# A product's sign, swap and add on GpSimd, handed out one piece per unit

## The chip, the cores and the metric

The kernel runs on one core of one Trainium2 chip. The metric is the device time of one execution in microseconds (us), the median of several runs. Before the change it was 2526.43 us in three runs (2524.81, 2526.43 and 2528.34).

## The reference

The kernel filters a signal and puts every filtered row through a small two-layer network. In the reference, cut to what matters:

```python
X = np.fft.rfft(x, axis=1)                 # x: (8, 3008, 256)
F = (filt_r + 1j * filt_i)[None, :, :]     # (1505, 256)
y = np.fft.irfft(X * F, n=3008, axis=1)
h = y.reshape(24064, 256) @ w_in           # w_in: 256 x 2048
P = a[0] + a[1] * h + a[2] * h**2 + a[3] * h**3
Q = 1.0 + abs(b[0]) * abs(h) + abs(b[1]) * h**2
out = (P / (Q + 1e-06)) @ w_out            # w_out: 2048 x 256
```

All data is float32.

## The kernel before, in words

**Two streams of work.** The network is cut into 752 units: 47 stretches of 512 rows, times 16 slices of 128 of the 2048 columns of `w_in`. The filter (a Fourier transform of length 3008 = 47 x 64 by matmuls) is cut into items, batch after batch: 16 first-stage matmuls (`s1`), 12 forward matmuls with a product by the filter (`y`, function `product`), 12 inverse matmuls (`z`, function `inverse`), and last-stage matmuls (`x`, function `stage3`). Batch 0 is done ahead of the units. The items of batches 1 to 7 are placed between the units, at most one in each.

**A unit.** Six matmuls make `h` in a bank of PSUM (L459, L460, L462). ScalarE, VectorE and GpSimd work on it over the next units. Six matmuls more (L536 to L538) put the two parts `hi` and `lo` of the result through `w_out`; they stand four, mostly five, units later in TensorE's order. Each engine does its instructions strictly in the order in which the function `pipeline` issues them. In unit `i` that is: the six matmuls of `h`; the matmul of a filter item if there is one; the six output matmuls; then the steps of the table `ORDER`, each with a lag (a lag of 2 is work on unit `i - 2`). The first three steps of the table (`CPOS = 3`) come ahead of the filter item's work on the other engines, the rest behind it. So within unit `i` VectorE does `g_hi` of unit `i - 2` (L513), then the item's work, then `rest`, `p` and `g_lo` (L521, L504, L527). GpSimd does the item's work, then `pool_m` of unit `i - 2` (L518, which reads `hi` of that unit), then `pool_q1` of unit `i - 1` (L499). These two are named m and q1 below.

**A product.** The forward matmul of an item `y` leaves a 128 x 512 tile in PSUM. VectorE multiplies it by the two parts of the filter (L354, L355). GpSimd then takes the halves of the first result, 64 partitions each, multiplies them by a column of signs and writes each to the other half of a tile `zw` (four instructions of 64 x 256, L366), and adds `zw` to the second result (one instruction, L371). The sum is the operand of the inverse matmul (L380).

**When an item's steps are issued.** The items are Python generators. `yield` with a cost ends an item; a bare `yield` ends its work in this unit, and the next unit goes on with it and takes no other item. `WAITS = (0, 1)` puts one such `yield` behind the fourth sign, so that before the change a product takes two units, and the add stands in the second. A new item starts when a credit, which grows by 0.6 (batch 1) or 0.38 (later) in each unit, is positive; the item's cost (1.2 for a product, 0.86 for an inverse, 0.62 for a first-stage matmul) is taken off. Behind product `i` stands the inverse of `i - 1`. The credit is capped at 2.5; it grows in the pause of at least four units ahead of the first product of a batch.

Of the kernel before, what the change touches and what calls it, by code (L numbers as in the profile page):

```python
# [9 lines left out]
F32 = mybir.dt.float32  # L10
# [4 lines left out]
ALU = mybir.AluOpType  # L15
# [12 lines left out]
C = 256  # L28
# [10 lines left out]
PGAP, XGAP = 1, 1  # L39
CPOS = 3  # L40
OG = 2
WAITS = (0, 1)
ORDER = [('g_hi', 2), ('act3', 1), ('act0', 0), ('act4', 1), ('act2', 0), ('act1', 0), ('rest', 3), ('p', 1), ('g_lo', 3), ('pool_m', 2), ('pool_q1', 1), ('pool_q0', 0)]
EV1, EV2, EVO = "A", "AV", "AV"
XB, FB = 4, 3
# [12 lines left out]
TT = 512  # L58
# [41 lines left out]
def conv_moe(ctx: ExitStack, tc: tile.TileContext, xp, fr, fi, w_in, w_out, ab, mats, a1, e, sgn, outT):  # L100
    nc = tc.nc
# [4 lines left out]
    conv = ctx.enter_context(tc.tile_pool(name="conv", bufs=2))  # L106
# [7 lines left out]
    sgn_sb = consts.tile([128, 32], F32, name="sgn_sb")[:, :K2]  # L114
# [38 lines left out]
    def inverse(y, x, t):  # L153
        v.reciprocal(y, x)
        tt(out=t, in0=x, in1=y, op=ALU.mult)
        ts(out=t, in0=t, scalar1=-1.0, scalar2=2.0, op0=ALU.mult, op1=ALU.add)
        tt(out=y, in0=y, in1=t, op=ALU.mult)
# [36 lines left out]
    class Weights:  # L194


        def __init__(self, i):
            self.i = i
            q, k = divmod(i, 4)
            self.out = k > 1  # L200
            if self.out:
                f = 2 * q + k - 2
                self.parts = wo_sb[:, f]
                self.src = wo32[f * 256 : f * 256 + 256].rearrange("(a p) c -> p a c", p=128)
            else:
                self.parts = wi_sb[:, q, k]
                self.src = wi32[k * 128 : k * 128 + 128, q * 1024 : q * 1024 + 1024].rearrange("p (a c) -> p a c", a=2)
# [52 lines left out]
    def evac(which, out, in_, i):  # L260
        if which[i % len(which)] == "A":
            nc.scalar.activation(out, in_, AF.Copy)
        else:
            nc.vector.tensor_copy(out, in_)
# [26 lines left out]
    def stage1(b, q, xin=None):  # L291
# [12 lines left out]
            rows(scr1[b])[:, 4 * q : 4 * q + 4, :].rearrange("r m c -> r (m c)"), ev.rearrange("p a b -> p (a b)")  # L304
        )

    class Stage2:


        def __init__(self, b):  # L310
            self.b, self.f, self.tin, self.ev, self.z = b, {}, {}, {}, {}

        def tl(self, tag, q, **kw):
            return conv.tile([128, 4, C], F32, tag=tag, name=f"{tag}{self.b}_{q}", **kw)
# [28 lines left out]
        def product(self, i):  # L343
            b, (q, j) = self.b, divmod(i, 2)
            yield COST[1]
            bank, yt = banks.tile(f"y_{b}_{i}")
            nc.tensor.matmul(yt, mats_sb[:, 0, :], self.flat(self.tin[q], j), start=True, stop=True)  # L347
            yield
            self.z[i] = z, z2 = [self.flat(f_, j) for f_ in self.f[q]]

            def signed(k):
                return slice(k * C, k * C + C), sgn_sb[:, 2 * i + k : 2 * i + k + 1]

            nc.vector.tensor_tensor(out=z2, in0=yt, in1=z2, op=ALU.mult)  # L354
            nc.vector.tensor_tensor(out=z, in0=yt, in1=z, op=ALU.mult)  # L355
            banks.done(bank, 0.5)
            if b == 0:

                return

            zw = conv.tile([128, TT], F32, tag="zw", name=f"zw{b}_{i}")
            for o, n in ((1, 0), (0, 1)):
                o_, n_ = slice(64 * o, 64 * o + 64), slice(64 * n, 64 * n + 64)
                for k in range(2):
                    cs, sg = signed(k)
                    nc.gpsimd.tensor_scalar(  # L366
                        out=zw[o_, cs], in0=z2[n_, cs], scalar1=sg[n_], scalar2=1.0, op0=ALU.mult, op1=ALU.mult
                    )
                if WAITS[n]:
                    yield  # L370
            nc.gpsimd.tensor_tensor(out=z, in0=z, in1=zw, op=ALU.add)  # L371

        def inverse(self, i):
            b, (q, j) = self.b, divmod(i, 2)
            if j == 0:
                self.ev[q] = self.tl("ev", q)
            yield COST[2]
            bank, zt = banks.tile(f"z_{b}_{i}")
            z, z2 = self.z.pop(i)
            nc.tensor.matmul(zt, mats_sb[:, 1, :], z, start=True, stop=b > 0)  # L380
            if b == 0:
                nc.tensor.matmul(zt, mats_sb[:, 2, :], z2, start=False, stop=True)
            yield
            evac(EV2 if b else "A", self.flat(self.ev[q], j), zt, i)
            banks.done(bank, 0.5)
# [154 lines left out]
    banks = None  # L540
# [14 lines left out]
    def conv_items(b):  # L555
        for q in range(8):
            yield from stage1(b, q)
        for _ in range(GAP):
            yield
        yield from stage2(b)  # L560

    def run(gen):
        for _ in gen:
            pass
# [84 lines left out]
    def pipeline(squares):  # L649


        n = nt * 16
        live = {}
        sp = ExitStack()
        gen, cost, credit, nxt = None, 0.0, 0.0, 1
        xgen, xk, xi = None, 2, 0
        active = None
        done, freed, ready = 0, -9, None
        last = -9
        for i in range(n + LAG + 2 * OG):  # L660
            t, f = divmod(i, 16)
            banks.now = i
            if i < n:
                live[i] = Unit(i, squares)

            def step(lag, *names):
                if 0 <= i - lag < n:
                    for name in names:
                        getattr(live[i - lag], name)()

            if i == 0:
                sp.enter_context(tc.manual_schedule(engines=HEAD_SP))
            if i == SPN:
                sp.close()
            if i < 16:
                for _ in range(3 if i == 0 else 1):
                    dec.load()
                for _ in range(HP[i]):
                    dec.step()
                while dec.done < i // 4 * 4 + 3:  # L680
                    dec.load()
                    dec.step()
            if f == 0 and xgen and T * (t + 1) > chunks[xk - 1][0] * G:
                run(xgen)
                xgen = active = None
            step(0, "product_in")

            credit = min(credit + RATES[nxt > 1], 2.5)
            post = []
            if i < n and f in (XF, XF + 8) and not xgen and xk < len(chunks):  # L690
                g0, g1 = chunks[xk]
                need = (g1 - 1) // NH
                if g1 * G <= t * T + RX and ((g0 if f > XF else g1) * G < T * (t + 2) or need < nxt):
                    if need >= nxt:
                        run(gen or conv_items(nxt))
                        gen, active = None, None
                        nxt += 1
                    xgen = stage3(xk)
                    xk += 1
                    next(xgen)  # L700
                    xi = i
            if xgen and i > xi and not active and i >= last + XGAP:
                next(xgen)
                post.append("x")
            elif credit > 0 and i < n and not active and i >= last + PGAP and not (xgen and i > xi):
                if gen is None and nxt < B and i >= SPN and i >= 94 * nxt - 94 - EARLY:
                    gen = conv_items(nxt)
                    cost = next(gen)
                if gen:
                    next(gen)  # L710
                    credit -= cost
                    post.append("c")

            for _ in range(2):
                if done < n and done <= i - LAG and (done % 16 or done == 0 or i >= freed + OG):
                    live.pop(done).product_out()
                    if done % 16 == 15:
                        ready = done // 16
                        freed = i
                    done += 1  # L720
                    if done > i - LAG - 1:
                        break
            for name, lag in ORDER[:CPOS]:
                step(lag, name)
            if post:
                active = post[0]
            if active:
                last = i
            if active == "x":
                if next(xgen, None) is None:  # L730
                    xgen = None
                active = None
            elif active:

                cost = next(gen, 0)
                if cost is not None:
                    active = None
                if cost == 0:
                    gen = None
                    nxt += 1  # L740
            for name, lag in ORDER[CPOS:]:
                step(lag, name)
            if ready is not None:
                mlp_out(ready, squares)
                ready = None

    with tc.manual_schedule(engines=ENGINES):
        banks = Banks(8 - T * 2 // TT)
# [71 lines left out]
```

## Time and profile before

| | before |
|---|---|
| median of three runs | 2526.43 us |
| profiled execution | 2528.11 us |
| its span, first to last instruction | 2526.3 us |
| mean granted TensorE clock | 0.991 |
| TensorE (PE) busy | 98% |
| VectorE (DVE) busy | 90% |
| ScalarE (ACT) busy | 87% |
| GpSimd (POOL) busy | 73% |

The profiled execution took 1.68 us more than the median. Of its 2528.11 us, 1.8 lie outside the span. A busy share is an average over the whole span; the profile's 40 slices of some 63 us each tell where an engine had room.

### The profile page before, as it was taken

The numbers are of one execution on the slowest core, as the hardware profiler recorded it, in microseconds if no ns is written. First come the engines' busy times: TensorE is split into PE (matmuls) and PEld (weight loads), VectorE is DVE, ScalarE is ACT, GpSimd is POOL, SyncE is SP. The second block draws the span as 40 slices with busy tenths as digits, with TensorE's granted clock in tenths as the row PEclk, the third lists the DMA queues.
The fourth block names the chain that finished last, engine by engine and source line by source line (L and its number), as shares of the span: only waits on it lengthen the run. The fifth ranks groups of instructions, "written<-read, shape, count | busy, mean of one in ns | idle before, by whom it ended". The sixth has DMA issues, their size and how long they took to land.

```text
span 2526.3 us, 35508 instructions
## 1 busy us (share of the span) xinstructions
PE 2466.2 (98%) x10456; PEld 1921.5 (76%) x10456; DVE 2265.1 (90%) x3573; ACT 2201.5 (87%) x4194; POOL 1851.5 (73%) x1984
## 2 busy tenths in 40 slices
PE   5699999999999999999999999999999999999998
PEld 1477777777777777878777777777777778888887
DVE  5789988999889998999889998899988999999998
ACT  4588889888898889888898889888898889999997
POOL 3568876887668876788668886688757887677776
PEclk8899999999999999999999999999999999999999
DMA  8643332222323222231322322222222211000000
GB/s 265 185 136 105 103 113 86 81 83 71 101 90 94 78 82 71 95 95 60 107 83 74 92 78 91 87 85 86 80 82 94 76 42 32 28 24 22 24 9 19
DMA packets 104364, 208.94 MB, mean 83 GB/s; under 512 B 9696, under 2 KB 59104, under 8 KB 104160
## 3 DMA queue, kind: packets, MB, share of 16 engines
q1 hardware_dynamic: 100944, 199.30, 25.8%
q10 hardware_dynamic: 3216, 7.27, 0.9%
q8 instruction: 85, 1.39, 0.2%
q14 instruction: 119, 0.97, 0.1%
HBM read 131.56 MB, written 74.97 MB: 82 GB/s over the span
## 4 chain that ended last, share of the span: by engine, by line
PE 91%; DVE 4%; DMA 1%; POOL 1%; ACT 1%; issue 1%; SPq 0%; ACTq 0%; DVEq 0%; POOLq 0%
PE o L537 13%; PE o L536 13%; PE o L538 13%; PE h_u L460 13%; PE h_u L459 13%; PE h_u L462 13%; PE x L425 4%; PE s L299 4%; PE y L347 3%; PE z L380 3%; DVE h_u L521 1%; DVE hi_u L513 1%; DVE h_u L504 1%; POOL zw L366 1%; POOL q_u L518 0%
## 5 line engine op out<-in xcount | busy, mean ns | idle before, releaser
L518 POOL TENSOR_TENSOR q_u<-q_u,hi_u 128x512 f32<-128x512 f32 x752 | 973.7, 1295 | 478.6 <-DVE hi_u L513 459.7
L536 PE MATMUL o<-hi_u,wo_sb 128*128 128x512 f32 x1504 | 703.8, 468 | 0.0
L467 ACT ACTIVATE q_u<-h_u 128x512 f32<-128x512 f32 x752 | 449.9, 598 | 209.3 <-PE h_u L462 138.9
L513 DVE SCALAR_TENSOR_TENSOR hi_u<-h_u,words_sb,a_u 128x512 fp32r<-128x512 f32 x752 | 561.5, 747 | 68.0 <-ACT a_u L489 66.2
L521 DVE SCALAR_TENSOR_TENSOR h_u<-h_u,words_sb,q_u 128x512 f32<-128x512 f32 x752 | 567.1, 754 | 59.9 <-POOL q_u L518 58.2
L459 PE MATMUL h_u<-xh,wi_sb 128*128 128x512 f32 x1504 | 595.1, 396 | 3.7 <-DVE xl L437 2.3
L537 PE MATMUL o<-lo_u,wo_sb 128*128 128x512 f32 x1504 | 590.6, 393 | 1.2 <-DVE lo_u L527 1.2
L538 PE MATMUL o<-hi_u,wo_sb 128*128 128x512 f32 x1504 | 588.3, 391 | 0.0
L460 PE MATMUL h_u<-xl,wi_sb 128*128 128x512 f32 x1504 | 587.9, 391 | 0.2
L499 POOL TENSOR_SCALAR q_u<-q_u,words_sb 128x512 f32<-128x512 f32 x752 | 579.5, 771 | 2.8 <-ACT a_u L484 2.8
L504 DVE SCALAR_TENSOR_TENSOR h_u<-w_u,words_sb,h_u 128x512 f32<-128x512 f32 x752 | 563.3, 749 | 3.4 <-ACT w_u L474 3.4
L527 DVE TENSOR_TENSOR lo_u<-h_u,a_u 128x512 fp32r<-128x512 f32 x752 | 516.4, 687 | 0.1
L484 ACT ACTIVATE a_u<-q_u 128x512 f32<-128x512 f32 x752 | 475.4, 632 | 0.4 <-DVE lo_u L527 0.4
L489 ACT ACTIVATE a_u<-a_u 128x512 f32<-128x512 f32 x752 | 470.3, 625 | 0.0
L480 ACT ACTIVATE q_u<-q_u 128x512 f32<-128x512 f32 x752 | 469.5, 624 | 0.0
L462 PE MATMUL h_u<-xh,wi_sb 128*128 128x512 f32 x1504 | 465.0, 391 | 0.0
L474 ACT ACTIVATE w_u<-h_u 128x512 f32<-128x512 f32 x752 | 443.8, 590 | 0.3 <-POOL wi_sb L245 0.3
L536 PEld LDWEIGHTS o<-hi_u,wo_sb 128*128 128x128 f32 x1504 | 282.6, 188 | 112.2 <-issue 64.5
L537 PEld LDWEIGHTS o<-lo_u,wo_sb 128*128 128x128 f32 x1504 | 282.9, 188 | 110.0 <-issue 59.8
L459 PEld LDWEIGHTS h_u<-xh,wi_sb 128*128 128x128 f32 x1504 | 282.7, 188 | 73.0 <-DVE lo_u L527 6.7
L460 PEld LDWEIGHTS h_u<-xl,wi_sb 128*128 128x128 f32 x1504 | 283.0, 188 | 63.9 <-issue 3.5
L538 PEld LDWEIGHTS o<-hi_u,wo_sb 128*128 128x128 f32 x1504 | 282.6, 188 | 61.5
(96 smaller groups left out, 1878.8 us busy)
## 6 DMA issues: line engine op xcount, KB each, us to landing
xin<-xp SPq DMA_DIRECT2D x64, 384.0 KB, 3.8
scr<-s1e SPq DMA_DIRECT2D x64, 384.0 KB, 4.0
xin<-scr SPq DMA_DIRECT2D x48, 512.0 KB, 5.1
scr<-ev SPq DMA_DIRECT2D x96, 256.0 KB, 3.8
tl<-scr SPq DMA_DIRECT2D x64, 384.0 KB, 3.1
outT<-oe SPq DMA_DIRECT2D x47, 512.0 KB, 3.0
f<-fr SPq DMA_DIRECT2D x87, 256.0 KB, 4.1
f<-fi SPq DMA_DIRECT2D x87, 256.0 KB, 3.9
```

Source lines behind the costliest of these rows:

```text
L459: nc.tensor.matmul(o, w_in_part(0, f, cc), xh[:, cc, ts], start=cc == 0, stop=False)
L460: nc.tensor.matmul(o, w_in_part(0, f, cc), xl[:, cc, ts], start=False, stop=False)
L462: nc.tensor.matmul(o, w_in_part(1, f, cc), xh[:, cc, ts], start=False, stop=cc == 1)
L499: nc.gpsimd.tensor_scalar(out=self.q, in0=self.q, scalar1=AIK, scalar2=SGN, op0=ALU.mult, op1=ALU.add)
L504: v.scalar_tensor_tensor(out=H, in0=w, scalar=PK, in1=H, op0=ALU.add, op1=ALU.mult)
L513: nc.vector.scalar_tensor_tensor(out=self.hi, in0=self.H, scalar=self.p0, in1=self.a, op0=ALU.add, op1=ALU.mult)
L518: nc.gpsimd.tensor_tensor(out=self.q, in0=self.q, in1=self.hi.bitcast(F32), op=ALU.mult)
L521: nc.vector.scalar_tensor_tensor(out=self.H, in0=self.H, scalar=self.p0, in1=self.q, op0=ALU.add, op1=ALU.subtract)
L527: nc.vector.tensor_tensor(out=self.lo, in0=self.H, in1=self.a, op=ALU.mult)
L536: nc.tensor.matmul(o, w_out_part(0, f, dd), self.hi, start=f == 0, stop=False)
L537: nc.tensor.matmul(o, w_out_part(0, f, dd), self.lo, start=False, stop=False)
L538: nc.tensor.matmul(o, w_out_part(1, f, dd), self.hi, start=False, stop=f == 15)
```

## The change

The four signs and the add are no longer issued by `product`. Behind VectorE's two multiplications `product` puts an entry into a list `pending`: the unit's number, the item, and three steps. Step 0 is two of the four signs (one half of the partitions), step 1 the two others, step 2 the add. `product` has no bare `yield` behind the multiplications any more, so it takes one unit, and the next unit is free for another item. In each unit, behind the first three steps of `ORDER` and ahead of the item's work, `pipeline` issues one step of the oldest entry, if that entry is from an earlier unit. And `inverse`, just ahead of its matmul, issues at once all the steps that are left of its own product (and of those ahead of it in the list).

```diff
-WAITS = (0, 1)
...
+    pending = []
+
+    def advance():
+        steps = pending[0][3]
+        steps.pop(0)()
+        if not steps:
+            pending.pop(0)
...
-            zw = conv.tile([128, TT], F32, tag="zw", name=f"zw{b}_{i}")
-            for o, n in ((1, 0), (0, 1)):
-                o_, n_ = slice(64 * o, 64 * o + 64), slice(64 * n, 64 * n + 64)
-                for k in range(2):
-                    cs, sg = signed(k)
-                    nc.gpsimd.tensor_scalar(
-                        out=zw[o_, cs], in0=z2[n_, cs], scalar1=sg[n_], scalar2=1.0, op0=ALU.mult, op1=ALU.mult
-                    )
-                if WAITS[n]:
-                    yield
-            nc.gpsimd.tensor_tensor(out=z, in0=z, in1=zw, op=ALU.add)
+            pending.append((banks.now, self, i, [lambda n=n: self.swap(i, z, z2, n) for n in range(3)]))
+
+        def swap(self, i, z, z2, n):
+            if n == 0:
+                self.zw[i] = conv.tile([128, TT], F32, tag="zw", name=f"zw{self.b}_{i}")
+            zw = self.zw[i]
+            if n == 2:
+                nc.gpsimd.tensor_tensor(out=z, in0=z, in1=zw, op=ALU.add)
+                return
+            o_, n_ = slice(64 - 64 * n, 128 - 64 * n), slice(64 * n, 64 * n + 64)
+            for k in range(2):
+                cs, sg = slice(k * C, k * C + C), sgn_sb[:, 2 * i + k : 2 * i + k + 1]
+                nc.gpsimd.tensor_scalar(
+                    out=zw[o_, cs], in0=z2[n_, cs], scalar1=sg[n_], scalar2=1.0, op0=ALU.mult, op1=ALU.mult
+                )
...
             yield COST[2]
+            while any(s is self and k == i for _, s, k, _ in pending):
+                advance()
             bank, zt = banks.tile(f"z_{b}_{i}")
...
             for name, lag in ORDER[:CPOS]:
                 step(lag, name)
+            if pending and pending[0][0] < i:
+                advance()
```

The number of instructions on each engine stays the same. What moves is shown at the start of batch 3, in units 186 to 193. On GpSimd `q_u187` is the tile of unit 187 that m and q1 work on, `zw3_0` the swapped tile of product 0 of batch 3, and `f13_0` the tile that the add writes. Before, from q1 of unit 186 on:

```order
L499 TENSOR_SCALAR q_u186_7062<-q_u186_7062,words_sb_81 128x512
L518 TENSOR_TENSOR q_u186_7062<-q_u186_7062,hi_u186_7142 128x512
L499 TENSOR_SCALAR q_u187_7111<-q_u187_7111,words_sb_81 128x512
L366 TENSOR_SCALAR zw3_0_7184<-f23_0_7066,sgn_sb_75 64x256 x4
L518 TENSOR_TENSOR q_u187_7111<-q_u187_7111,hi_u187_7175 128x512
L499 TENSOR_SCALAR q_u188_7146<-q_u188_7146,words_sb_81 128x512
L371 TENSOR_TENSOR f13_0_7065<-f13_0_7065,zw3_0_7184 128x512
```

After, from the same instruction on:

```order
L509 TENSOR_SCALAR q_u186_7082<-q_u186_7082,words_sb_81 128x512
L528 TENSOR_TENSOR q_u186_7082<-q_u186_7082,hi_u186_7146 128x512
L509 TENSOR_SCALAR q_u187_7117<-q_u187_7117,words_sb_81 128x512
L377 TENSOR_SCALAR zw3_0_7194<-f23_0_7037,sgn_sb_75 64x256 x2
L528 TENSOR_TENSOR q_u187_7117<-q_u187_7117,hi_u187_7187 128x512
L509 TENSOR_SCALAR q_u188_7150<-q_u188_7150,words_sb_81 128x512
L377 TENSOR_SCALAR zw3_0_7194<-f23_0_7037,sgn_sb_75 64x256 x2
L372 TENSOR_TENSOR f13_0_7036<-f13_0_7036,zw3_0_7194 128x512
L377 TENSOR_SCALAR zw3_1_7234<-f23_0_7037,sgn_sb_75 64x256 x2
L528 TENSOR_TENSOR q_u188_7150<-q_u188_7150,hi_u188_7227 128x512
```

The second pair of signs now stands behind m of unit 187 and q1 of unit 188, with the add right behind it and two signs of the next product behind that.

On TensorE the inverse matmul of the same product, `z_3_0`, stood in unit 193 before, three units behind the add:

```order
L459 MATMUL h_u193_7305<-xh_612,wi_sb_76 128x512
L460 MATMUL h_u193_7305<-xl_613,wi_sb_76 128x512
L459 MATMUL h_u193_7305<-xh_612,wi_sb_76 128x512
L460 MATMUL h_u193_7305<-xl_613,wi_sb_76 128x512
L462 MATMUL h_u193_7305<-xh_612,wi_sb_76 128x512 x2
L380 MATMUL z_3_0_7314<-f13_0_7065,mats_sb_78 128x512
```

After, it stands in unit 190, the unit in which the add is issued:

```order
L469 MATMUL h_u190_7209<-xh_612,wi_sb_76 128x512
L470 MATMUL h_u190_7209<-xl_613,wi_sb_76 128x512
L469 MATMUL h_u190_7209<-xh_612,wi_sb_76 128x512
L470 MATMUL h_u190_7209<-xl_613,wi_sb_76 128x512
L472 MATMUL h_u190_7209<-xh_612,wi_sb_76 128x512 x2
L390 MATMUL z_3_0_7219<-f13_0_7036,mats_sb_78 128x512
L546 MATMUL o11_0_6926<-hi_u185_7113,wo_sb_77 128x512
```

The forward matmul `y_3_0` moved from unit 189 to 188, and `y_3_1` from 191 to 189; the output matmuls of unit 185 stand right behind the inverse. Counted over the order of all units: before, each of the 84 inverse matmuls of batches 1 to 7 stands 2 to 10 units behind the unit in which its add is issued. After, 7 stand in the same unit (`z_1_0` in unit 29, `z_1_1` in 31, `z_1_11` in 63, `z_3_0` in 190, `z_4_0` in 281, `z_6_0` in 463, `z_7_0` in 554), 4 one unit behind it, 73 two or more. In six of the seven, all but `z_1_1`, the product's forward matmul stands two units ahead of the inverse, and every unit from it to the inverse has an item.

## Rows read from the trace of the kernel before

**Rows 1.** The page's first two parts: busy time of the engines with the share of the span and the number of instructions, and the 40 slices of TensorE's busy share and of its granted clock in tenths.

```profile
PE 2466.2 (98%) x10456; PEld 1921.5 (76%) x10456; DVE 2265.1 (90%) x3573; ACT 2201.5 (87%) x4194; POOL 1851.5 (73%) x1984
...
PE   5699999999999999999999999999999999999998
...
PEclk8899999999999999999999999999999999999999
```

**Rows 2.** Busy time of each engine in three stretches that lie behind the start: us, then PE, PEld, DVE, ACT and POOL busy with the number of instructions, the granted clock, and the share and rate of the DMA engines.

```profile
130.00:400.00 270.00, 269.79 (x1128) 205.53 (x1127) 236.72 (x372) 234.33 (x448) 202.00 (x221) 1.00 0.37 109
400.00:2050.00 1650.00, 1649.49 (x7043) 1290.18 (x7042) 1495.49 (x2335) 1460.52 (x2793) 1248.51 (x1358) 1.00 0.27 84
2050.00:2500.00 450.00, 450.00 (x2023) 372.46 (x2022) 429.78 (x676) 427.07 (x822) 332.95 (x331) 1.00 0.07 24
```

**Rows 3.** Groups of instructions on GpSimd: line, engine, operation, names, shapes, count, then busy us and mean ns of one, then idle us before them and what ended it.

```profile
L518 POOL TENSOR_TENSOR q_u<-q_u,hi_u 128x512 f32<-128x512 f32 x752 | 973.7, 1295 | 478.6 <-DVE hi_u L513 459.7
L499 POOL TENSOR_SCALAR q_u<-q_u,words_sb 128x512 f32<-128x512 f32 x752 | 579.5, 771 | 2.8 <-ACT a_u L484 2.8
L366 POOL TENSOR_SCALAR zw<-f,sgn_sb 64x256 f32<-64x256 f32 x336 | 156.5, 476 | 120.7 <-issue 53.1 <-DVE f L354 51.7 <-POOL q_u L499 7.8
L371 POOL TENSOR_TENSOR f<-f,zw 128x512 f32<-128x512 f32 x84 | 108.7, 1294 | 0.0
```

**Rows 4.** Waits: who waited for whom, us in total, times, longest.

```profile
DVE h_u L521 <- POOL q_u L518: 58.2, 124, 1.0
```

**Rows 5.** Instructions in order of time around the product `y_3_0`, which is in unit 189 before (737.97 is the first matmul of that unit, 741.58 that of unit 190): start us, duration us, engine, line, operation, names, shapes, count, and in brackets the idle time before and what ended it.

```profile
736.13 0.74 DVE L513 SCALAR_TENSOR_TENSOR hi_u<-h_u,words_sb,a_u 128x512 fp32r<-128x512 f32 x1
...
737.03 1.30 POOL L518 TENSOR_TENSOR q_u<-q_u,hi_u 128x512 f32<-128x512 f32 x1 [3.16 <-DVE hi_u L513]
...
737.97 0.39 PE L459 MATMUL h_u<-xh,wi_sb 128*128 128x512 f32 x1
...
738.31 0.77 POOL L499 TENSOR_SCALAR q_u<-q_u,words_sb 128x512 f32<-128x512 f32 x1
...
739.33 1.02 PE L347 MATMUL y<-xin,mats_sb 128*128 128x512 f32 x2
...
739.68 0.74 DVE L513 SCALAR_TENSOR_TENSOR hi_u<-h_u,words_sb,a_u 128x512 fp32r<-128x512 f32 x1
...
740.39 0.69 DVE L354 TENSOR_TENSOR f<-y,f 128x512 f32<-128x512 f32 x1
...
740.99 0.68 DVE L355 TENSOR_TENSOR f<-y,f 128x512 f32<-128x512 f32 x1
...
741.24 1.96 POOL L366 TENSOR_SCALAR zw<-f,sgn_sb 64x256 f32<-64x256 f32 x4 [2.15 <-issue]
...
741.58 0.39 PE L459 MATMUL h_u<-xh,wi_sb 128*128 128x512 f32 x1
...
743.50 0.74 DVE L513 SCALAR_TENSOR_TENSOR hi_u<-h_u,words_sb,a_u 128x512 fp32r<-128x512 f32 x1
```

**Rows 6.** The same view of TensorE in unit 193, which has the inverse matmul `z_3_0`.

```profile
750.66 0.39 PE L459 MATMUL h_u<-xh,wi_sb 128*128 128x512 f32 x1
...
752.02 1.02 PE L380 MATMUL z<-f,mats_sb 128*128 128x512 f32 x2
...
754.27 0.40 PE L459 MATMUL h_u<-xh,wi_sb 128*128 128x512 f32 x1
```

**Rows 7.** The same view in batch 1, where items stand densest: a forward matmul and the first signs behind it.

```profile
256.32 1.02 PE L347 MATMUL y<-xin,mats_sb 128*128 128x512 f32 x2
...
259.30 1.95 POOL L366 TENSOR_SCALAR zw<-f,sgn_sb 64x256 f32<-64x256 f32 x4 [0.57 <-DVE f L354]
```

**Rows 8.** The same view of TensorE in the first 120 us: three matmuls that waited.

```profile
72.57 1.10 PE L380 MATMUL z<-fxh,mats_sb 128*128 128x512 f32 x2 [1.66 <-issue]
...
80.01 1.10 PE L380 MATMUL z<-fxh,mats_sb 128*128 128x512 f32 x2 [2.05 <-ACT wi_sb L243]
...
116.16 0.50 PE L459 MATMUL h_u<-xh,wi_sb 128*128 128x512 f32 x1 [2.34 <-DVE xl L437]
```

**Rows 9.** Stretches behind the first two of these waits and behind the third, in the columns of rows 2; the granted clock is the third figure from the end, as a share of full speed.

```profile
73.00:76.00 3.00, 3.00 (x8) 1.33 (x7) 1.96 (x4) 2.19 (x3) 1.07 (x3) 1.00 0.71 235
79.80:83.00 3.20, 2.99 (x7) 1.44 (x8) 3.03 (x6) 0.60 (x1) 2.41 (x2) 1.00 0.83 298
117.40:120.60 3.20, 2.41 (x9) 1.91 (x8) 3.02 (x5) 1.51 (x4) 2.96 (x3) 0.50 0.08 23
120.80:124.00 3.20, 3.16 (x7) 1.88 (x7) 3.18 (x6) 3.12 (x6) 2.91 (x3) 0.50 0.82 251
```

**Rows 10.** DMA issues of the page: names, queue, operation, count, KB each, median us from issue to landing.

```profile
xin<-scr SPq DMA_DIRECT2D x48, 512.0 KB, 5.1
...
f<-fr SPq DMA_DIRECT2D x87, 256.0 KB, 4.1
```

More of the change, by code (lines that the diff above doesn't have):

```diff
@@ L305, in stage1 @@
         )
+    pending = []
[4 more added lines that the diff above has]
+            pending.pop(0)
     class Stage2:
         def __init__(self, b):
-            self.b, self.f, self.tin, self.ev, self.z = b, {}, {}, {}, {}
+            self.b, self.f, self.tin, self.ev, self.z, self.zw = b, {}, {}, {}, {}, {}
         def tl(self, tag, q, **kw):
@@ L349, in product @@
             self.z[i] = z, z2 = [self.flat(f_, j) for f_ in self.f[q]]
-            def signed(k):
-                return slice(k * C, k * C + C), sgn_sb[:, 2 * i + k : 2 * i + k + 1]
             nc.vector.tensor_tensor(out=z2, in0=yt, in1=z2, op=ALU.mult)
```

## The prediction, made before the changed kernel ran

> **What bounds the kernel now.** I read the page's busy shares and slices first. TensorE is busy 98% of the span, and in every slice behind the first few it is at 90% or more, at full granted clock [rows 1]. The 60 us in which it is not busy lie almost wholly in the start, in which batch 0 is done and which the change doesn't touch. The stretches behind 130 us say it more sharply: of 2370 us TensorE was busy 269.79 + 1649.49 + 450.00 = 2369.28, at a granted clock of 1.00 [rows 2]. So from there on the time is the length of TensorE's own queue of matmuls. Two things follow. A wait that another engine loses buys nothing: all the waits of TensorE there are worth 0.7 us. And a wait that TensorE gains is paid in full, because nothing behind it runs faster than its own pace to catch up.
>
> GpSimd is busy 73% and waits 459.7 us for `hi` alone [rows 1, 3]. It isn't the bound. What matters is how late in a unit it finishes, once TensorE waits for it.
>
> **The change part by part.**
>
> *Instructions.* None is added or removed: 336 signs of 476 ns and 84 adds of 1294 ns stay [rows 3], as do all matmuls. This part costs 0.
>
> *Pieces spread over units.* Before, four signs stand in one piece (1.96 us, [rows 5]) ahead of m, which makes m late and with it VectorE's `rest`, which waits 58.2 us in all for m [rows 4]. After, at most a pair usually stands there, and these waits shrink. They are hidden behind TensorE now, so I take 0, with 0.7 us [rows 2] as the most that it can give back.
>
> *Items that come earlier.* The pause of one unit behind a product goes, so forward matmuls stand up to four units earlier and in places in two units running. The loads for them move too, on SP's queue and in their issue. A load lands in 5.1 us or less [rows 10], while the filter and the data of a product are asked for several units of 2.7 us or more ahead, and no wait for a DMA is left behind 130 us [rows 2]: 0, and if that cover were gone, some 5 us once. A second cost is the PSUM bank: an item now often gets the bank that the product one unit ahead leaves. VectorE's second multiplication ends at 740.99 + 0.68 = 741.67, and the next item's matmul is due 3.61 behind 739.33, at 742.94 [rows 5]. That leaves 1.27 us. In batch 1 VectorE is later: the signs start 2.98 behind the matmul (259.30 - 256.32, [rows 7]) and not 1.91 (741.24 - 739.33, [rows 5]), so 1.07 less is left, still 0.2. I take 0, and up to 2 us for the top of the range.
>
> *The inverse that no longer has room.* This is the term that counts. In six places the inverse matmul stands two units behind its product's forward matmul, and `inverse` issues the last pair of signs and the add in that same unit. TensorE must wait for them. I work it out at `z_3_0` on the clock of rows 5, where unit 189 before stands for unit 188 after: both hold `y_3_0` and follow two units with last-stage matmuls.
>
> TensorE: a unit with such an item takes 741.58 - 737.97 = 3.61 [rows 5], the inverse's own unit too (754.27 - 750.66 = 3.61), and the inverse starts 752.02 - 750.66 = 1.36 into it [rows 6]. So it is due at 737.97 + 3.61 + 3.61 + 1.36 = 746.55.
>
> GpSimd, unit 188: `hi` ends at 739.68 + 0.74 = 740.42; m follows 0.16 behind it (737.03 against 736.13 + 0.74), at 740.58; q1 starts 1.28 behind m (738.31 - 737.03) and takes 0.77, to 742.63. Unit 189: the first pair of signs, about half of 1.96, to 743.61. Then m has to wait for the next `hi`, 743.50 + 0.74 = 744.24, and starts at 744.40; q1 ends 1.28 + 0.77 later, 746.45. Unit 190: the second pair to 747.43, the add (1.29) to 748.72. A handover to TensorE of 0 to 0.16, as from `hi` to m: I take 0.1. So TensorE starts at 748.8 and has waited 2.2 us.
>
> The chain turns on `hi`, which comes behind VectorE's two multiplications and so behind the forward matmul itself; it is much the same at the five other places. Bounds: nothing, if GpSimd were wholly done by then, and 3.3 us, if VectorE is 1.07 later, as in rows 7. I take 2.2, since rows 5 are the very pattern. Six places: 13.2 us.
>
> The seventh, `z_1_1`, has one more unit, and TensorE has by then just waited at `z_1_0`: 2.2 us in which the others catch up. The same sum puts its add within 0.1 us of the due time. The four inverses one unit behind their add have a unit more still. I take 0 for these five, up to 1 us each for the top.
>
> *The clock.* A wait of 2.2 us has a second price. At the start, waits of 1.66 and 2.05 us left the granted clock at 1.00, which is 2.4 GHz; behind one of 2.34 us it was 0.50, 1.2 GHz, in two stretches of 3.2 us [rows 8, 9]. 2.2 lies between. 3.2 us at half clock cost TensorE 1.6 us of work, and it has no room to make that up. Bounds: no place loses the clock, 0; all six, each for both stretches, 6 x 3.2 = 19.2. I take two of six, one stretch each: 3.2 us.
>
> The Trainium skill, page "TensorE: Matmul & The Clock Gate", section "HAM oscillation — how this bites in real kernels", has it that the clock falls only behind idle gaps longer than one that it names, and 2.2 us is shorter. By it this term would be 0. The trace does not bear it out, since the clock fell behind 2.34 us; it is a rival below.
>
> *Sum.* 13.2 + 3.2 = 16.4 us on the profiled execution's 2528.11, that is 2544.5. That execution took 1.7 more than the median, so against the median of the runs 2526.43 + 16.4 = 2543 us, 0.65% slower.
>
> **The rivals.** *The clock holds at all six.* For it: it held behind 1.66 and 2.05 us. Against: 2.34 us. Time: 2526.4 + 13.2 = 2540 us. By the skill's rule this would be the outcome.
>
> *The clock falls at most places, or the waits are nearer 3.* For it: rows 7 and 9. Five drops of 1.6 us, or 0.6 us more for each wait and two drops: 2526.4 + 13.2 + 8 = 2548, or 2526.4 + 16.8 + 3.2 = 2546; taken together, about 2550 us.
>
> *Not slower: GpSimd is there in time.* The change takes the block of four signs away ahead of m. If by that VectorE and GpSimd run so far ahead that the second pair stands ready to start by 744.2 in place of 746.45, the add ends at 746.5, the six waits vanish, and the 0.7 us of TensorE's other waits is all that is left to change: 2526 us. It decides from about 0.8 us for each wait, 5 us in all. Against it: in the chain above GpSimd has nothing ahead of it that the change could still remove; m is held by `hi`, and `hi` by the forward matmul.
>
> *The change does what it says only in part.* That the step per unit doesn't hold in seven places is the forecast's own ground; if the order's rows did not count because the wait is attached elsewhere, the time would again be 2526 us. That goes with the rival before.
>
> **How the numbers follow.** Forecast, six waits of some 2.2 us and one to three drops of the clock: 0.48, with a range of its own of 2539 to 2547. Clock holds: 0.22. Most places lose the clock, or waits near 3 us: 0.18. Not slower or barely: 0.12. Within 0.2% means 5 us to either side, about what a measurement of this kernel tells from no change. Faster by more than that needs 5 us where TensorE's waits hold 0.7, so 0.02 is enough; the rest of the last case, 0.10, is "same"; 0.88 is slower. The range leaves the last case out, and a little of the dear one: 2534 to 2551 us.
>
> **What would show it.** In the profile of the changed kernel: inverse matmuls (L390) with an idle time before them ended by GpSimd's add (L372), six of about 2 us; at these places the add ends within 0.2 us of the inverse's start; behind some of them a stretch of granted clock 0.50 and the mean clock below 0.991; TensorE's waits elsewhere as before; VectorE's wait for m below 58.2 us. Wrong would be: no wait of an inverse for GpSimd, a wait of about 1 us or of 3, TensorE waiting for VectorE or a DMA instead, or a time within 5 us of 2526.

## The result and the profile after

The changed kernel took 2544.36 us, the median of six runs (2541.54 to 2547.32), against 2526.82 us for the kernel before, run beside it (six runs, 2524.81 to 2529.31). The ratio is 1.0067, with a 95% interval of 1.0057 to 1.0077. That is 17.5 us slower; 2543 us were forecast, with a range of 2534 to 2551. The profiled execution took 2545.24 us, with a span of 2543.0 us.

The page of the changed kernel, in the lines of [rows 1]:

```profile
PE 2468.9 (97%) x10456; PEld 1922.0 (76%) x10456; DVE 2260.9 (89%) x3573; ACT 2201.3 (87%) x4194; POOL 1852.5 (73%) x1984
...
PE   5699999999999999999999999999999999999998
...
PEclk8899999999999999999999999999999999999999
```

No engine has more instructions and hardly one has more busy time, TensorE 2.7 us. The slices show nothing: a slice is 64 us long, and what was lost lies in pieces of a few us. The stretches of [rows 2] show it:

```profile
130.00:400.00 270.00, 264.84 (x1100) 200.79 (x1101) 231.07 (x364) 229.60 (x439) 200.16 (x220) 1.00 0.37 108
400.00:2050.00 1650.00, 1641.36 (x6997) 1282.61 (x6996) 1483.31 (x2322) 1450.93 (x2774) 1239.31 (x1345) 1.00 0.27 84
2050.00:2500.00 450.00, 450.00 (x2021) 371.53 (x2020) 427.19 (x672) 425.46 (x818) 331.93 (x333) 1.00 0.07 24
```

TensorE is now idle for 5.16 + 8.64 + 0 = 13.8 us of the 2370, where it was idle for 0.72. The third stretch lost nothing. The clock reads 1.00 in all three, since two decimals of a long mean hide a few us at half speed.

The view of waits of the changed kernel says who was waited for:

```profile
PEld z L390 <- POOL f L372: 16.0, 7, 2.6
...
PE z L390 <- POOL f L372: 12.9, 6, 2.2
...
DVE h_u L531 <- POOL q_u L528: 3.8, 16, 0.9
```

Six inverse matmuls wait for GpSimd's add, 2.2 us at most, 12.9 of the 13.8 us in all. (The weight loads, which stand ahead of the matmuls, count a seventh.) VectorE's wait for m, 58.2 us in [rows 4], is down to 3.8. So the change did what it says on GpSimd, gave VectorE 54 us, and none of them reached the end.

The groups of GpSimd that answer to [rows 3]:

```profile
L377 POOL TENSOR_SCALAR zw<-f,sgn_sb 64x256 f32<-64x256 f32 x336 | 156.4, 476 | 16.5 <-POOL q_u L509 0.7
L372 POOL TENSOR_TENSOR f<-f,zw 128x512 f32<-128x512 f32 x84 | 108.8, 1295 | 0.5
```

Count and duration are the same. The idle time ahead of the signs fell from 120.7 to 16.5 us: their operand is now there when they come up.

Where the time goes at one of the six places shows in the instructions around `z_3_0`, in the columns of [rows 5]:

```profile
746.68 0.74 DVE L523 SCALAR_TENSOR_TENSOR hi_u<-h_u,words_sb,a_u 128x512 fp32r<-128x512 f32 x1
...
747.57 1.31 POOL L528 TENSOR_TENSOR q_u<-q_u,hi_u 128x512 f32<-128x512 f32 x1 [0.75 <-DVE hi_u L523]
...
748.38 0.39 PE L469 MATMUL h_u<-xh,wi_sb 128*128 128x512 f32 x1
...
748.86 0.77 POOL L509 TENSOR_SCALAR q_u<-q_u,words_sb 128x512 f32<-128x512 f32 x1
...
749.72 0.94 POOL L377 TENSOR_SCALAR zw<-f,sgn_sb 64x256 f32<-64x256 f32 x2
...
750.75 1.27 POOL L372 TENSOR_TENSOR f<-f,zw 128x512 f32<-128x512 f32 x1
...
752.07 0.77 PE L390 MATMUL z<-f,mats_sb 128*128 128x512 f32 x1 [2.15 <-POOL f L372]
```

TensorE begins unit 190 at 748.38 and is due at the inverse 1.36 later [rows 6], at 749.74. The second pair of signs only starts then. It stands behind m and q1, and m behind `hi`. The add ends at 752.02, the inverse starts at 752.07, 2.33 us late. The bracket says 2.15 because the record of the matmul before it ends at 749.92, later than the inverse was due.

The last sign of the price is the granted clock, in the columns of [rows 9], behind the inverses at 752.07 and 1646.94:

```profile
752.70:755.90 3.20, 3.20 (x8) 2.20 (x7) 1.15 (x2) 2.17 (x5) 3.02 (x5) 0.50 0.00 0
756.20:759.40 3.20, 3.20 (x13) 2.26 (x13) 0.95 (x2) 1.91 (x5) 3.14 (x3) 1.00 0.57 157
1646.90:1650.10 3.20, 3.16 (x6) 1.84 (x7) 1.08 (x2) 1.05 (x3) 2.94 (x4) 0.50 0.00 0
```

At 0.50, the lower level of 1.2 GHz, TensorE got through 8 matmuls in a stretch in which it gets through 13 at 1.00. Behind the four other inverses the clock stayed at 1.00. The account, from the distance between the first matmuls of neighbouring units: six units longer by 2.40 to 2.46 us, 14.5 in all; the unit of `z_1_1` by 0.35; two half-clock stretches, 1.6 each, 3.2. That is 18.0 us. Other small lengthenings of units behind the start, which came to 4.1 us before, are 1.8 us less. The balance is 16.2, and the spans differ by 16.7: up to unit 8 (138.07 us before, 139.20 after) 1.1 more were needed, and behind the start of the last unit 0.7 less.

### The profile page after: what moved, and what is told of

The parts are those of the page before. It is cut to its first block, busy times and chain, and to the rows that moved or that the text cites. A ratio compares the mean times of both kernels' runs of the same rounds, so it can differ in the third digit from the quotient of the medians.

```text
span 2543.0 us, 35594 instructions
## 1 busy us (share of the span) xinstructions
PE 2468.9 (97%) x10456; PEld 1922.0 (76%) x10456; DVE 2260.9 (89%) x3573; ACT 2201.3 (87%) x4194; POOL 1852.5 (73%) x1984
## 4 chain that ended last, share of the span: by engine, by line
PE 91%; DVE 3%; ACT 2%; DMA 2%; issue 1%; POOL 1%; SPq 0%; ACTq 0%; POOLq 0%; DVEq 0%
PE o L547 13%; PE o L546 13%; PE o L548 13%; PE h_u L470 13%; PE h_u L469 13%; PE h_u L472 13%; PE x L435 4%; PE s L298 4%; PE z L390 3%; PE y L354 3%; DMA scr<-s1e 1%; DVE hi_u L523 1%; DVE h_u L531 0%; DVE h_u L514 0%; DMA f<-fi 0%
```

## The experiments

The theory: the loss is the six inverses whose product's pieces are issued so late that the add ends behind the inverse's due time. The rivals: that items stand closer, or that pieces are spread over units, costs by itself. All kernels are the changed one with one edit, and each group is compared with the kernel before on the same chip (medians 2526.01 to 2527.51).

**All three steps in the unit behind the product.** Items and matmuls stay where the change put them; only the pieces come sooner.

```diff
-            if pending and pending[0][0] < i:
+            while pending and pending[0][0] < i:
                 advance()
```

> All three steps of a product are issued in the unit behind it, ahead of m; the items stand in the same units as in the changed kernel, and no add stands in its inverse's unit (the nearest are 6 that stand one unit ahead of it). Theory (the time went into inverses that wait for pieces issued too late): at z_3_0 four signs and the add run from 1.14 us into unit 189 to about 4.4, that is 0.7 us into unit 190, and the inverse is due at 1.36: no wait, 2527 us (2525 to 2529), ratio 1.000. Rival A (items packed closer cost by themselves: VectorE late, banks, loads): 2540 to 2545, as the changed kernel, since the items stand where they stand there.

Measured: 2526.19 us, ratio 0.9991 (0.9982 to 1.0). No inverse waits for an add. Around `z_3_0` in this kernel:

```profile
739.03 1.96 POOL L377 TENSOR_SCALAR zw<-f,sgn_sb 64x256 f32<-64x256 f32 x4
...
741.08 1.31 POOL L372 TENSOR_TENSOR f<-f,zw 128x512 f32<-128x512 f32 x1
742.33 1.29 POOL L528 TENSOR_TENSOR q_u<-q_u,hi_u 128x512 f32<-128x512 f32 x1
742.88 1.02 PE L390 MATMUL z<-f,mats_sb 128*128 128x512 f32 x2
```

The add ends at 742.39, ahead of its inverse, which has no bracket. The whole loss is gone with items as close as in the changed kernel, so with the pieces there in time the closeness costs nothing.

**The spreading alone.** The pause of one unit behind a product comes back; the pieces stay spread.

```diff
             pending.append((banks.now, self, i, [lambda n=n: self.swap(i, z, z2, n) for n in range(3)]))
+            yield
```

> The pieces are handed out over the three units behind as in the changed kernel, but the product keeps its second unit, so that all items stand in the units in which they stood before. One inverse (z_1_11) has only its add issued in its own unit, seven have it one unit ahead. Theory: one wait of about 1.7 us, none at the seven: 2528 us (2526 to 2530), ratio 1.001. Rival A (packing): 2527. Rival B (handing out costs by itself): 2535 or more.

Measured: 2527.7 us, ratio 0.9997 (0.9988 to 1.0006), with one wait of an inverse left, 1.4 us, `z_1_11`. Spreading alone is no cost either. But for this one place, only the two together bring an inverse to its product's unfinished pieces.

**The inverse held until its pieces are issued.** Spreading and closeness stay; a new item isn't started while the pieces of its product are in the list.

```diff
...
+            self.want = i
             yield COST[2]
+            self.want = None
...
-            elif credit > 0 and i < n and not active and i >= last + PGAP and not (xgen and i > xi):
+            elif credit > 0 and i < n and not active and i >= last + PGAP and not (xgen and i > xi) and not any(
+                s.want == k for _, s, k, _ in pending
+            ):
```

> As the changed kernel, but an inverse is not started while a piece of its product is still to be issued, so no piece is ever issued in its inverse's unit; 15 adds stand one unit ahead of it. Products still take one unit. Theory: no wait for the add, 2527 us (2525 to 2530). Rival A (packing): between, 2530 to 2540, since items still stand closer than before. Rival B (handing out): 2535 or more.

Measured: 2526.42 us, ratio 0.9993 (0.9984 to 1.0002), and no wait of TensorE for the add. Taking away the issue in the inverse's own unit takes away the loss.

**Two steps behind the product, one later.** If the theory holds, the price should go with how late the add is.

```diff
             if pending and pending[0][0] < i:
+                if len(pending[0][3]) == 3:
+                    advance()
                 advance()
```

> As the changed kernel, but both pairs of signs are issued in the unit behind the product; at the six places only the add is left for the inverse's unit. Items stand as in the changed kernel. From its trace at z_3_0: four signs from 1.14 to 3.05 us in unit 189, m to 4.4, q1 to 5.15, which is 1.52 into unit 190, the add to 2.9, the inverse at 3.04 in place of 1.36: a wait of 1.7 us, and none at z_1_1. Theory: six waits, 10.1 us, and no drop of the clock behind waits this short: 2537 us (2535 to 2539). Theory with the clock falling behind a third of such waits: 2540. Rival A (packing): 2540 to 2545, as the changed kernel.

**All steps one unit later.** The other way:

```diff
-            if pending and pending[0][0] < i:
+            if pending and pending[0][0] < i - 1:
                 advance()
```

> As the changed kernel, but the first step comes two units behind the product, not one: at the six places all four signs and the add are left for the inverse's unit, and five more inverses (z_1_1, z_1_4, z_4_11, z_5_0, z_5_1) have their add issued in their own unit. Theory: six waits of 3.4 us (20 us), five of 1 to 2.3 us (7 us), and the clock falls behind most of the six, 1.6 us or more each (10 us): 2564 us (2555 to 2575). Without any price of the clock: 2554. Rival A (packing): 2540 to 2545, since the items stand as in the changed kernel.

Measured: 2533.42 us for the first (ratio 1.003, 1.002 to 1.0039) and 2560.45 for the second (1.0136, 1.012 to 1.0151). Their views of waits, the first kernel's:

```profile
PE z L390 <- POOL f L372: 7.2, 6, 1.5
```

and the second's:

```profile
PE z L390 <- POOL f L372: 24.4, 11, 3.2
```

With the changed kernel and the first experiment that makes a series:

| steps in the unit behind the product | waits of inverses for the add | time against before |
|---|---|---|
| three | none | -1.3 us |
| two | 6, 7.2 us | +7.3 us |
| one | 6, 12.9 us | +17.5 us |
| none, one later each | 11, 24.4 us | +34.3 us |

The time follows the waits. With two steps the clock fell behind none of the six inverses in the one execution that was profiled, and the loss is about the waits alone (the six units are 8.8 us longer). With all steps one unit later the eleven units are some 32 us longer, three drops of the clock among them: two of the six places, where most of the six were expected, and `z_4_11`. The expectation of 2537 was too dear: at three of the six places the unit grew by 1.3 us only, at the others by 1.6 to 1.7.

**The five instructions in the product's own unit.** This was meant to test closeness alone, with the block where the kernel before has its signs:

```diff
-            pending.append((banks.now, self, i, [lambda n=n: self.swap(i, z, z2, n) for n in range(3)]))
+            for n in range(3):
+                self.swap(i, z, z2, n)
```

> The five GpSimd instructions of a product are issued in the product's own unit again, but without the pause of a unit behind it: the items stand as in the changed kernel, the pieces earlier than in the kernel before. Theory: the add ends some 2 us ahead of each inverse, no wait: 2527 us (2525 to 2529). VectorE waits for m more often than before, hidden. Rival A (packing): 2540 to 2545. Rival B (handing the pieces out over units costs by itself): 2527 here too.

Measured: 2572.46 us, ratio 1.0169 (1.0155 to 1.0183). The expectation was wrong by 45 us. The view of waits of this kernel:

```profile
DVE h_u L532 <- POOL q_u L529: 128.5, 85, 2.8
PEld h_u L470 <- DVE lo_u L538: 48.1, 75, 2.1
...
PE h_u L470 <- DVE lo_u L538: 15.3, 20, 1.7
```

TensorE waits not for the add but for VectorE's `lo`, which frees the bank of a unit; VectorE waits for m. In the kernel before, the same weight loads waited 6.7 us:

```profile
PEld h_u L459 <- DVE lo_u L527: 6.7, 17, 1.0
```

That is 41 us more, most of the 45 that were lost; the matmuls' own records, with 15.3 us, show less of it. In order of time, in the kernel with the block ahead of m:

```profile
751.01 0.74 DVE L524 SCALAR_TENSOR_TENSOR hi_u<-h_u,words_sb,a_u 128x512 fp32r<-128x512 f32 x1
751.72 0.69 DVE L358 TENSOR_TENSOR f<-y,f 128x512 f32<-128x512 f32 x1
...
752.57 1.96 POOL L378 TENSOR_SCALAR zw<-f,sgn_sb 64x256 f32<-64x256 f32 x4 [2.14 <-issue]
...
754.62 1.29 POOL L373 TENSOR_TENSOR f<-f,zw 128x512 f32<-128x512 f32 x1
...
755.87 1.30 POOL L529 TENSOR_TENSOR q_u<-q_u,hi_u 128x512 f32<-128x512 f32 x1
...
762.63 0.76 DVE L532 SCALAR_TENSOR_TENSOR h_u<-h_u,words_sb,q_u 128x512 f32<-128x512 f32 x1 [2.76 <-POOL q_u L529]
...
764.69 0.50 PE L470 MATMUL h_u<-xh,wi_sb 128*128 128x512 f32 x1 [0.73 <-DVE lo_u L538]
```

`hi` ends at 751.75, and m could start 0.16 later. But the block stands ahead of m in GpSimd's order, and it waits for VectorE's multiplication behind `hi`, which ends at 752.41. GpSimd is idle for 2.14 us up to 752.57 (the view names no releaser here; that it was the multiplication is read from the order of times), then works through 3.3 us of block, and m starts at 755.87, 4 us late. With products in neighbouring units the lateness adds up, until VectorE idles for 2.76 us and TensorE runs out of banks.

**The same block behind m.** If that reading holds, the block should be nearly free in the same unit once m stands ahead of it. The list stays, and is emptied behind the step that issues m. (`e2_pack` stands for the kernel just shown.)

```diff
-            if pending and pending[0][0] < i:
-                advance()
...
             for name, lag in ORDER[CPOS:]:
                 step(lag, name)
+                while name == 'pool_m' and pending:
+                    advance()
```

> As e2_pack, the five instructions in the product's own unit and the items as in the changed kernel, but behind m and ahead of q1, not ahead of m. In e2_pack the signs wait for VectorE until 3.27 us into the unit and end at 6.6, and m comes only behind them; here m is done at 3.9, and signs and add run from 3.9 to 7.2. Theory (e2_pack lost its 45 us because m, and with it lo and the bank of a later h, came late; the place ahead of m while the operand is not there yet is what costs): 2527 us (2525 to 2531). Rival (3.25 us of GpSimd in one unit are too much wherever they stand): 2550 to 2572.

**The signs in the product's unit, the add in the next.** The place that the signs had before, and no pause.

```diff
-            pending.append((banks.now, self, i, [lambda n=n: self.swap(i, z, z2, n) for n in range(3)]))
+            self.swap(i, z, z2, 0)
+            self.swap(i, z, z2, 1)
+            pending.append((banks.now, self, i, [lambda: self.swap(i, z, z2, 2)]))
```

> Signs in the product's own unit ahead of m and the add in the next, as in the kernel before, but the product doesn't hold that next unit, so the items stand as in the changed kernel. At z_3_0 the add ends some 0.2 us behind the inverse's due time, and a second product stands in the unit of the add. Theory: m late by 4 us in the unit of the signs and by 2 us more where products follow each other; six waits of 0.2 us and TensorE waiting for lo in the dense places: 2532 us (2527 to 2545), between the kernel before and e2_pack. Rival (the packing of the items is harmless with any order of the pieces): 2527.

Measured: 2529.24 us (1.001, 1.0001 to 1.0019) and 2531.87 us (1.0023, 1.0014 to 1.0032). So of the 45 us of the block ahead of m, about 3 are left behind m, and about 6 with the add moved on. The place in the order decides, not the 3.3 us of work; and ahead of m the block costs nothing either once its operands are there, as in the first experiment.

**The changed kernel twice more.** For the clock, which one execution can't settle.

> The changed kernel once more, for the number of its clock drops in another execution. Theory: the same seven waits (2.4 us six times, 0.3 us once), 0 to 4 of them with a stretch of granted clock 0.50 behind, and the span follows their number with 1.6 us each: 2539.8 us with none, 2543.0 with two. Rival (the two drops belong to the places, not to chance): again at z_3_0 and z_6_0.

> As again_1: one more execution of the changed kernel, span 2539.8 us plus 1.6 for each drop of the clock behind an inverse.

Measured: 2544.25 and 2546.93 us. The six waits are the same, but the places of the half clock aren't, so the rival, as it was put, is out. In the second of them, behind `z_1_0`, `z_1_11`, `z_3_0`, `z_6_0` and `z_7_0`:

```profile
213.90:217.10 3.20, 3.20 (x9) 2.52 (x8) 0.75 (x1) 2.29 (x5) 3.02 (x5) 0.50 0.00 0
333.30:336.50 3.20, 3.20 (x6) 1.87 (x7) 1.36 (x3) 0.42 (x1) 1.76 (x2) 0.50 0.58 166
753.70:756.90 3.20, 3.20 (x12) 2.35 (x13) 1.77 (x3) 2.06 (x5) 3.00 (x5) 1.00 0.00 0
1647.40:1650.60 3.20, 3.20 (x8) 2.02 (x7) 1.35 (x3) 1.92 (x4) 3.02 (x6) 0.50 0.00 0
1947.80:1951.00 3.20, 3.20 (x6) 1.88 (x7) 1.01 (x3) 1.19 (x3) 3.02 (x5) 0.50 0.01 3
```

That makes four drops; the first of them had three, the profiled execution two. `z_6_0` lost the clock in all three, `z_4_0` in none. The seventh wait, at `z_1_1`, was there in the profiled execution alone: in both others the clock fell at `z_1_0` just ahead of it. The spans, 2542.0 and 2544.7, are less than the expectation gives for three and four drops (2544.6 and 2546.2); it left out the start, which differs from one execution to another (first matmul of unit 0 at 101.06 and 102.88, against 104.28 us in the profiled one).

## Why the prediction was right

- *What bounds.* Right. VectorE's waits for m fell by 54 us and gave nothing; TensorE's idle time grew by 13.1 us and was paid in full. (Of the slices of [rows 1], the last is below 90% too, not only the first few. What it lacks lies behind 2500 us, where the stretches of [rows 2] end.)
- *Instructions, spreading, closer items, loads and banks at 0.* Right, and shown apart: three steps in the unit behind (closeness) and the spreading with the pause are both at the time before. No matmul of TensorE waits for a bank or a DMA behind 130 us in the changed kernel. The 5.1 us of [rows 10] were read as the longest time to landing; they are a median, and the longest of those 48 loads took 10.7 us. That the cover of the banks is thin, as the 1.27 and 0.2 us of the prediction say, fits the block ahead of m, where a late m made TensorE wait for banks at 20 places.
- *The six waits.* Right in place, number and chain, a little too small: 2.40 to 2.46 us of lengthening where 2.2 was taken. The sum itself came to 2.25 and was rounded down. It left out that GpSimd didn't start the next instruction at once: in the rows around `z_3_0` 0.09 us pass between q1 and the signs (749.63 to 749.72) and again between signs and add (750.66 to 750.75). Against that, the handover was 0.05 and not 0.1, and signs and add took 0.06 less than was taken. That is about the 2.33 at this place. The remaining 0.1 of a longer unit lies in the inverse itself: at `z_4_0` the output matmul behind it starts 0.56 us after it (1051.20 to 1051.76), and 0.45 in the kernel with all three steps in the unit behind (1039.18 to 1039.63).
- *The seventh.* 0.35 us where 0 to 0.1 was taken. With the six, 14.8 us measured for 13.2.
- *The clock.* Two drops of 1.6 us, as taken, but by luck in the number: repeated executions show three and four. Place by place a drop cost 1.45 to 1.66 us: the unit of `z_3_0` took 7.64 and 7.48 us in the two executions with a drop there and 6.03 in the one without, that of `z_7_0` 7.72 with one and 6.07 and 6.09 without. By the rule of the Trainium skill, page "TensorE: Matmul & The Clock Gate", section "HAM oscillation — how this bites in real kernels", gaps as short as these leave the clock up. The trace disagrees, with 0.50 behind idle gaps of 2.14 and 2.15 us. The rival in which the clock holds, 2540 us, lies below all six runs; with the waits as they came it would give 2541.6, about the time of the fastest, so these times alone don't rule it out. In each of the three profiled executions the clock fell.
- *The sum.* 16.4 us forecast, 17.1 between the two profiled executions (2545.24 - 2528.11). The waits were 1.6 too cheap. About 1.8 us of small lengthenings that went made up for it, so that the total is closer than its terms; 0.5 us of start and end and 0.4 outside the span come on top. I had taken 0.7 us as the most that could go, from TensorE's idle time alone; what the 1.8 us were isn't known.
- *Not slower.* It needed GpSimd to be ahead by the second unit. It wasn't, since m is held by `hi` there: GpSimd idles 0.75 us ahead of m (747.57) and is late all the same.

## What to carry to other kernels

A piece of work that is issued at its consumer's place, because it was put off too long, costs all of its chain that is still left when the consumer is due; count, for each consumer, how many units lie between the first piece and the consumer before spreading over so many. Spreading gains nothing where the engine that is relieved waits on the bound anyway: here the same items with the pieces together one unit behind ran as fast as before, but no version was clearly faster. On an in-order engine a block belongs behind the instruction that the bounding chain needs, or where its operands are already there: the same five instructions in the product's own unit cost 45 us ahead of m, where their operand came later than m's, and 3 behind it; ahead of m one unit later, with the operand there, they cost nothing.

## What the runs showed of the hardware

A longer wait didn't make a drop of the clock surer. In the kernel with all steps one unit later the inverses waited some 3.2 us at the six places, and at four of them the clock stayed at 1.00; behind a shorter wait it fell. The matmul `z_3_0` of that kernel:

```profile
757.25 0.70 PE L390 MATMUL z<-f,mats_sb 128*128 128x512 f32 x1 [3.17 <-POOL f L372]
```

One behind a shorter wait:

```profile
1236.44 0.99 PE L390 MATMUL z<-f,mats_sb 128*128 128x512 f32 x1 [1.87 <-POOL f L372]
```

and the stretches behind the two:

```profile
758.00:764.00 6.00, 6.00 (x25) 4.39 (x24) 2.72 (x5) 5.28 (x10) 5.07 (x8) 1.00 0.00 1
...
1236.80:1240.00 3.20, 3.20 (x7) 1.86 (x6) 1.68 (x3) 0.52 (x1) 1.56 (x2) 0.50 0.09 23
```

What decides at which place it falls stays open: the same kernel with the same waits lost it at two, three and four places in three executions, so the length of the wait alone isn't it. Behind the six waits of 1.0 to 1.5 us of the kernel with two steps it fell at none, in one execution. A forecast can put a number of drops and 1.6 us each on such waits, with the whole count as the range.
